# A planned attention and MLP-mixer kernel: first scores of four heads together, pads on VectorE, token mix ahead of the next attention, the last u added by TensorE

## The chip, the cores and the metric

One core of a Trainium2 chip. The metric is the device time of one execution in microseconds (us). A profile shows a span some 2 us shorter than the time of the same execution; both are used below and told apart. For each execution the records give the mean clock that TensorE (PE) was granted, as a share of full speed.

## The reference, cut to what matters

```python
# q, k, v: (8, 8, 576, 64); block-causal mask in blocks of 64 positions
scores = scale * np.matmul(q, k.transpose(0, 1, 3, 2))
scores = np.where(block_i >= block_j, scores, -1e9)
attn = softmax(scores)
x = concat_heads(np.matmul(attn, v))                      # (8, 576, 512)
# mixer
h  = np.maximum(x.transpose(0, 2, 1) @ w_tok1, 0) @ w_tok2     # 576 -> 256 -> 576
u  = x + h.transpose(0, 2, 1)
return u + np.maximum(u @ w_ch1, 0) @ w_ch2                    # 512 -> 1536 -> 512
```

Batch by batch: attention gives x, the *token mix* gives u, the *channel mix* gives the output. 576 rows are four and a half tiles of 128, so the half tiles of two batches are joined into "mixed" tiles (`um`, `gm`). The mixed tile of the last two batches is the last work of the kernel.

## The kernel before

Every operation is handed to a planner (`Plan`). It holds a cost model, a priority per operation (lower first) and the pools of PSUM banks, and fixes, when the program is built, the order in which each engine runs its instructions. At run time each engine goes through its list in order. So a changed priority or cost can move instructions that the diff doesn't touch.

PSUM holds two score buffers of two banks each (`sc`), each used by one score pass at a time, and four banks for everything else (`mm`):

```python
    sc = ring(2, [128, 2, 512], FP32, "sc", psum)
    mm = ring(4, [128, 512], FP32, "mm", psum)
    ...
    WARM, KEEP = 16, 110
```

Constant parts of buffers are written once ("pads"). Those of v are on POOL (GpSimd), which also issues many of the loads:

```python
        for i in range(2):
            fill(
                "POOL", ("v", i), 3.0 + i,
                (v1[i][64:128, 4, :, :], 0.0),
                (v1[i][:, 0:4, :, 64:65], 1.0),
                (v1[i][0:64, 4, :, 64:65], 1.0),
            )
            fill("DVE", ("e", i), -1e3, (e_sb[i][:, :, 1536:1600], 0.0))
```

PE multiplies zeros while it has nothing to do: 16 matmuls at the start, then up to 110 *dummy matmuls*, each placed only if the planner finds a free bank of `mm` and an idle PE before 20 us. 13 of them find a place:

```python
        for n in range(KEEP):
            # one 256-column matmul on zeros into a bank of mm
            P.add("PE", 0.11, emit, pads["zeros"], 1e6, take=[(BANK, bank)], give=[bank], at=5.0 + 0.12 * n, until=20.0)
```

The attention of batch 0 handles two heads at a time (j = 0 to 3), each in three score passes:

```python
        for j in range(4):
            ...
            tails = first_tail(hg, heads, ready[hg], prio + 0.05)
            for n, s in enumerate((2, 1, 0)):
                op = score_set(0, parts, heads, ready[hg], prio + 0.1 * n, [note])   # 4 or 8 matmuls, one sc buffer
                ex = exp(dst, width, op, note, prio + 0.1 * n, urgent=2)             # ACT, 1024 wide
                exps.append(ex)
                for c in MASKS[s]:
                    exps.append(mask(e, c, hs, [ex], prio, urgent=1))                # DVE
```

The last block (the mixed tile of the last two batches) runs in two halves of 256 columns. Each has its own bank, an add of u on VectorE (DVE), and two stores of 64 KB:

```python
    def last_down(gt, ut, deps, prio):
        for f in range(2):
            cols = slice(256 * f, 256 * f + 256)
            # 12 matmuls of 256 columns into a bank
            op = P.add("PE", mm_cost(256, NDC), emit, deps + reuse(("o", f)), prio + 0.1 * f, take=[(BANK, bank)])
            # DVE: o_sb[f][:, 0, 0:256] = bank + ut[:, cols]
            op = P.add("DVE", dve_cost(256), emit, [op], prio, give=[bank])
            for kk in range(2):
                # store 64 rows x 256 columns, on SP's queue for kk = 0, on ACT's for kk = 1
```

The softmax here doesn't subtract the row's maximum and nothing guards it: scores larger than these inputs give would overflow.

## Time and profile before

| | before |
|---|---|
| time, median (4 runs of the comparison) | 314.57 us (314.33 to 315.25) |
| span in the profile, granted clock | 312.5 us, 0.996 |
| first score matmul to last exponential of batch 0 | 8.16 to 20.96 us |
| first 8-matmul scores of batch 1 on PE ("front" ends) | 27.77 us |
| from there to the start of PE's last block ("middle") | 276.85 us |
| from there to the end of the span ("tail") | 7.87 us |

The three last rows sum to the span: 27.77 + 276.85 + 7.87 = 312.49. The lines of the profile are shown in the prediction.

### The profile page before, as it was taken

What the parts mean: (1) busy time and instruction counts of PE and PEld (TensorE: products, weight loads), DVE (VectorE), ACT (ScalarE), POOL (GpSimd) and SP (SyncE); (2) the same over time, 40 slices, a digit from 0 to 9 for tenths busy, and PEclk for the clock granted to TensorE, in tenths of its full rate; (3) what the DMA queues carried; (4) which work ended last, traced back from release to release, by engine and by line L of the source; (5) the groups of instructions that cost most, each with busy time, mean ns of one, the idle gap of its engine ahead of it and who ended that gap; (6) DMA issues with size and microseconds to landing.
All of it is one profiled execution on the core that took longest, in us unless ns stands there. A gap on an engine that the chain in (4) does not pass through costs nothing.

```text
span 312.5 us, 7109 instructions
## 1 busy us (share of the span) xinstructions
PE 299.8 (96%) x2979; PEld 155.3 (50%) x3011; DVE 161.1 (52%) x374; ACT 163.3 (52%) x230; POOL 64.5 (21%) x102
## 2 busy tenths in 40 slices
PE   8898999999999999999999999999999999999993
PEld 3474436454555554553553556544444644444642
DVE  6967739798696586597393753434024022011022
ACT  4875872577757756758646867104504503604500
POOL 7966436612601502500400000000000000000000
PEclk9999999999999999999999999999999999999998
DMA  7999999997995998930890003032311313011013
GB/s 237 173 178 207 205 223 185 230 199 121 103 142 92 125 146 126 216 24 15 81 136 35 36 2 67 2 134 52 67 67 68 69 67 101 2 67 67 2 67 102
DMA packets 57023, 33.12 MB, mean 106 GB/s; under 512 B 43872, under 2 KB 47584, under 8 KB 56992
## 3 DMA queue, kind: packets, MB, share of 16 engines
q0 software_dynamic: 36960, 18.52, 45.3%
q1 hardware_dynamic: 19584, 13.44, 16.3%
q10 hardware_dynamic: 448, 0.72, 0.7%
q8 instruction: 23, 0.38, 0.5%
q14 instruction: 8, 0.07, 0.1%
HBM read 35.85 MB, written 9.44 MB: 145 GB/s over the span
## 4 chain that ended last, share of the span: by engine, by line
PE 64%; issue 12%; DVE 6%; DMA 5%; POOL 2%; POOLq 0%; DVEq 0%
PE mm L943 24%; PE mm L842 23%; PE sc L448 5%; PE mm L496 3%; PE mm L750 3%; DMA qraw<-in_q_dram 3%; PE mm L656 3%; PE mm L869 3%; DMA v<-in_v_dram 2%; DVE x_sb L524 1%; DVE kT L348 1%; DVE o_sb L959 1%; DMA out_dram<-o_sb 1%; POOL kraw L326 1%; POOL qraw L326 1%
## 5 line engine op out<-in xcount | busy, mean ns | idle before, releaser
L468 ACT ACTIVATE e_sb<-sc 128x1024 bf16<-128x1024 f32 x96 | 93.3, 1025 | 35.1 <-PE sc L448 33.1
L842 PE MATMUL mm<-uT,wc_sb 128*128 128x512 bf16 x384 | 88.9, 379 | 0.8 <-DVE u_sb L771 0.4
L943 PE MATMUL mm<-wc_sb,gT 128*128 128x512 bf16 x366 | 85.7, 379 | 1.8 <-issue 0.6
L642 ACT ACTIVATE gT<-mm 128x512 bf16<-128x512 f32 x76 | 45.4, 597 | 70.9 <-PE mm L842 70.7
L959 DVE TENSOR_TENSOR o_sb<-mm,u_sb 128x512 f32<-128x512 f32 x32 | 22.1, 690 | 83.5 <-PE mm L943 83.4
L842 PEld LDWEIGHTS <-wc_sb 128*128 128x128 bf16 x384 | 36.4, 98 | 46.3 <-issue 4.9
L943 PEld LDWEIGHTS <-gT 128*128 128x128 bf16 x384 | 36.0, 98 | 43.7 <-issue 4.1
L448 PE MATMUL sc<-qT,kT 32*128 32x64 bf16 (+4 forms) x752 | 36.3, 281 | 2.1 <-DVE qT L348 1.1
L496 PEld LDWEIGHTS <-e_sb 128*128 128x128 bf16 x896 | 31.1, 97 | 9.3 <-issue 4.8
L496 PE MATMUL mm<-v,e_sb 128*128 128x65 bf16 x896 | 33.4, 193 | 0.2
L377 POOL DMA_DIRECT2D v<-in_v_dram x30 | 25.3, 862 | 33.1 <-PE mm L496 30.9
L524 DVE TENSOR_TENSOR x_sb<-mm,rinv 128x320 bf16<-128x320 f32 x64 | 30.5, 488 | 1.4
L771 DVE TENSOR_TENSOR u_sb<-mm,x_sb 128x512 bf16<-128x512 f32 x32 | 20.6, 684 | 7.5 <-PE mm L750 3.7
L448 PEld LDWEIGHTS <-kT 32*128 32x128 bf16 x752 | 12.9, 93 | 20.3 <-issue 17.0
L348 DVE STREAM_TRANSPOSE kT<-kraw 128x576 int32<-128x576 int32 (+1 forms) x20 | 20.1, 1026 | 4.6 <-PE sc L448 3.0
L348 DVE STREAM_TRANSPOSE qT<-qraw 128x576 int32<-128x576 int32 (+1 forms) x20 | 20.1, 1025 | 0.5 <-DMA qraw<-in_q_dram 0.3
L644 DVE TENSOR_SCALAR gT<-mm 128x512 bf16<-128x512 f32 x20 | 13.7, 687 | 12.6 <-PE mm L842 12.4
L750 PE MATMUL mm<-aT,w_sb 128*128 128x512 bf16 x72 | 19.2, 380 | 0.3 <-DVE e_sb L474 0.2
L656 PE MATMUL mm<-x_sb,w_sb 128*128 128x512 bf16 (+1 forms) x99 | 17.9, 314 | 0.5 <-DVE x_sb L524 0.2
L326 POOL DMA_DIRECT2D kraw<-in_k_dram x15 | 8.4, 559 | 38.0 <-DVE kT L348 21.8
L474 DVE MEMSET e_sb<- 64x128 uint32 (+1 forms) x72 | 10.6, 153 | 9.7 <-ACT e_sb L468 6.1
L642 ACT ACTIVATE aT<-mm 128x512 bf16<-128x512 f32 (+1 forms) x15 | 8.1, 540 | 13.9 <-PE mm L656 13.9
(66 smaller groups left out, 182.1 us busy)
## 6 DMA issues: line engine op xcount, KB each, us to landing
out_dram<-o_sb SPq DMA_DIRECT2D x16, 512.0 KB, 2.8
kraw<-in_k_dram POOLq DMA_DIRECT2D x15, 288.0 KB, 6.3
qraw<-in_q_dram POOLq DMA_DIRECT2D x15, 288.0 KB, 6.6
v<-in_v_dram POOLq DMA_DIRECT2D x24, 128.0 KB, 5.5
wc_sb<-in_moe_w_ch_dram POOLq DMA_DIRECT2D x8, 192.0 KB, 7.8
wc_sb<-in_moe_w_ch_dram POOLq DMA_DIRECT2D x3, 512.0 KB, 11.2
gT<-in_v_dram POOLq DMA_DIRECT2D x9, 128.0 KB, 6.0
gT<-in_v_dram POOLq DMA_DIRECT2D x4, 256.0 KB, 13.3
```

Source lines behind the costliest of these rows:

```text
L348: nc.vector.transpose(dst[:, 0:S, :] .rearrange("p s e -> p (s e)") .bitcast(I32) .rearrange("p (a k) -> p k a", k=NB)[:, k0:k1], raw2.bit ...
L377: nc.gpsimd.dma_start(out=dst, in_=src)
L448: nc.tensor.matmul(out=sc[SC.index(notes[n // 2]["pool"])][:, n % 2, c0 : c0 + w], lhsT=kT[i][r, j0 : j0 + 128, par], rhs=qT[i][r, i0 : i0 ...
L468: nc.scalar.activation(dst, sc[SC.index(note["pool"])][:, :, 0:n], EXP, scale=scale)
L496: nc.tensor.matmul(out=u[:, I, 0:65], lhsT=w, rhs=vt[:, J, head, 0:65], start=(J == 0), stop=(J == I),)
L524: nc.vector.tensor_tensor(out=xt[:, :, 64 * head : 64 * head + 64], in0=u[:, :, 0:64], in1=ri.to_broadcast([128, 5, 64]), op=MULT,)
L642: nc.scalar.activation(dst, src, RELU)
L656: nc.tensor.matmul(out=bank_of(bank)[:, w * n : w * n + w], lhsT=wt[:, 128 * tt : 128 * (tt + 1)], rhs=xt[:, c, cols], start=(c == 0), sto ...
L750: nc.tensor.matmul(out=bank_of(bank), lhsT=w2_sb[:, t, c0 : c0 + 128], rhs=at[:, t, :], start=(t == 0), stop=(t == NDT - 1),)
L842: nc.tensor.matmul(out=bank_of(bank), lhsT=wc1_sb[:, m, 128 * cc : 128 * (cc + 1)], rhs=uT[b % 2][:, :, m, :], start=(m == 0), stop=(m == ...
L943: nc.tensor.matmul(out=bank_of(bank), lhsT=gt[:, cc, c0 : c0 + 128], rhs=wc2_sb[:, cc, :], start=(cc == 0), stop=(cc == NDC - 1),)
L959: nc.vector.tensor_tensor(out=o_sb[oi][:, n % 2, :], in0=bank_of(bank), in1=ut if mixed else ut[:, si, :], op=ADD,)
```

## The change

Its intent: batch 0's attention, where ACT is the engine that sets the pace, should start with more scores ready; POOL should issue loads instead of writing constants; the token mix of a batch should come before the next batch's attention in PE's order; and the end should not wait for an output buffer.

```diff
@@ init_tiles @@
             fill(
-                "POOL", ("v", i), 3.0 + i,
+                "DVE", ("v", i), -60 + 20 * i,
...
-            fill("DVE", ("e", i), -1e3, (e_sb[i][:, :, 1536:1600], 0.0))
+            fill("DVE", ("e", i), -70, (e_sb[i][:, :, 1536:1600], 0.0))
... (the other pads on DVE likewise: -1e3 becomes -70)
@@ Plan: a bank can be given back without the planner's usual lag; the dummies do @@
-                    heapq.heappush(gives, (o.end + lag, note["pool"], note["slot"]))
+                    heapq.heappush(gives, (o.end + lag * (not o.quick), note["pool"], note["slot"]))
...
             P.add(
                 "PE", 0.11, emit, pads["zeros"], 1e6, take=[(BANK, bank)], give=[bank], at=5.0 + 0.12 * n, until=20.0,
+                quick=True,
             )
@@ first_attention: first pass for four heads, heads 2 and 3 into banks of mm @@
-            tails = first_tail(hg, heads, ready[hg], prio + 0.05)
...
+                if j == 0 and n == 0:
+                    note = {}
+                    early = [{}, {}]
+                    op = score_set(
+                        0, parts, range(4), ready[hg], prio - 0.05, [(SC, note)] + [(BANK, x) for x in early]
+                    )
+                if j == 1 and n == 0:
+                    these = []
+                    for h, x in zip(heads, early):
+                        # ACT: one exponential of 512 from bank x
+                        these.append(P.add("ACT", act_cost(512), emit, [op0], prio, give=[x], urgent=2))
...
+                if n == (1 if j else 2):
+                    tails = first_tail(hg, heads, [op] + ready[hg], prio + 0.1 * n + 0.05)
... (one cast of the first k moves to the engine that the planner picks; load costs restated;
     the exponentials of the tails get the priority -3001)
@@ token_mix @@
-        prio = -500 + 10 * b
+        prio = -990.5 + 10 * b
...
-            prio = 1
+            prio = 0.5
@@ last_down: one bank of 512 columns, u added by TensorE @@
+            nc.tensor.matmul(out=bank_of(bank), lhsT=ident, rhs=ut, start=True, stop=False)
+            for cc in range(NDC):
+                nc.tensor.matmul(out=bank_of(bank), lhsT=gt[:, cc, :], rhs=wc2_sb[:, cc, :],
+                                 start=False, stop=(cc == NDC - 1))
...
+        oi = out_n[0] % 3                       # the third output buffer, free long before
+        for f, engine in enumerate(EVAC):       # two copies of 256 columns, DVE and ACT
+            cast(o, o_sb[oi][:, 0, cols], bank_of(bank)[:, cols])
+        for kk in range(2):                     # two stores of 128 KB instead of four of 64 KB
+            queue.dma_start(out=out[B - 2 + kk, 512:576, :], in_=o_sb[oi][64 * kk : 64 * kk + 64, 0, :])
```

## The prediction

> **What bounds the kernel now.** I read four views in this order: the busy shares on the profile page, the busy time of the engines in three stretches, the order of instructions in time at both ends, and the list of what TensorE (PE) waited for.
>
> The page's first part, then the stretches (columns: stretch in us, its length, busy us of PE, PEld, DVE, ACT and POOL, granted clock, DMA share, GB/s):
>
> ```profile
> PE 299.8 (96%) x2979; PEld 155.3 (50%) x3011; DVE 161.1 (52%) x374; ACT 163.3 (52%) x230; POOL 64.5 (21%) x102
> ...
> 20.00:28.00 8.00, 6.83 (x128) 5.63 (x128) 5.76 (x16) 4.22 (x9) 3.80 (x8) 1.00 1.13 205
> 28.00:305.00 277.00, 272.90 (x2651) 139.09 (x2675) 138.58 (x304) 144.46 (x198) 43.65 (x61) 1.00 0.60 97
> 305.00:313.00 8.00, 2.40 (x23) 1.91 (x20) 1.42 (x3) 0.00 (x0) 0.00 (x0) 0.82 0.31 99
> ```
>
> From 28 to 305 us PE is busy 272.9 of 277 us at full clock; no other engine is above 53% there. So the time is three pieces: a front of 28 us until PE is full, a middle that is PE's own stream plus 4.1 us of gaps, and a tail of 8 us. Busy PE in the first 20 us is no proof of useful work (dummy matmuls on zeros are counted), so I looked at the front in order of time (start, length, engine, line, what, idle time before it and its releaser):
>
> ```profile
> 10.74 1.80 POOL L250 MEMSET v<- 64x528 bf16 x6
> 12.52 2.02 POOL L396 DMA_DIRECT2D w_sb<-in_moe_w_tok_dram  x3
> ...
> 17.05 3.91 ACT L468 ACTIVATE e_sb<-sc 128x1024 bf16<-128x1024 f32 x4
> 17.74 0.59 POOL L326 DMA_DIRECT2D qraw<-in_q_dram  x1
> ...
> 24.93 1.26 DVE L348 STREAM_TRANSPOSE kT<-kraw 128x288 int32<-128x288 int32 x2 [0.88 <-DMA kraw<-in_k_dram]
> 26.45 1.26 DVE L348 STREAM_TRANSPOSE qT<-qraw 128x288 int32<-128x288 int32 x2 [0.27 <-DMA qraw<-in_q_dram]
> 27.56 0.68 DVE L717 CAST uT<-mm 128x512 bf16<-128x512 f32 x1
> 27.77 0.63 PE L448 MATMUL sc<-qT,kT 32*128 32x512 bf16 x8 [1.12 <-DVE qT L348]
> ```
>
> The reader is to see two chains. ACT runs exponentials without a gap from 8.83 to 20.96 us; what follows (values, token mix of batch 0) ends on PE at 26.65. Then PE stands 1.12 us because the next scores, which come first in its fixed order, need the q of batch 1. That load was issued at 17.74 and is in only at about 26.4. Behind q's transposes on DVE the last uT copy starts at 27.56 too. The loads are late because POOL, which issues them, spent 10.74 to 12.54 on six memsets, and the DMA engines ran dry behind it:
>
> ```profile
> 12.00:13.00 1.00, 0.97 (x16) 0.49 (x16) 0.90 (x3) 1.00 (x4) 0.94 (x4) 1.00 0.58 115
> 13.00:14.00 1.00, 0.67 (x11) 0.23 (x11) 0.90 (x6) 1.00 (x3) 1.00 (x3) 1.00 0.05 10
> 14.00:15.00 1.00, 0.88 (x20) 0.61 (x20) 0.90 (x4) 1.00 (x3) 0.93 (x3) 1.00 1.01 129
> ```
>
> Before and after this hole the DMA share is 1.0 or more, so the hole, (1-0.58)+(1-0.05) = 1.4 us, is pushed onto every later load. The tail:
>
> ```profile
> 304.62 2.78 PE L899 MATMUL mm<-wc_sb,gmT 128*128 128x256 bf16 x24
> 306.13 0.42 DVE L910 TENSOR_TENSOR o_sb<-mm,um_sb 128x256 f32<-128x256 f32 x1 [0.56 <-PE mm L899]
> 306.59 2.94 ACTq L918 DMA_DIRECT2D out_dram<-o_sb  x2
> 308.57 0.42 DVE L910 TENSOR_TENSOR o_sb<-mm,um_sb 128x256 f32<-128x256 f32 x1 [2.02 <-DMA out_dram<-o_sb]
> ```
>
> PE has finished at 307.40, yet the last add starts at 308.57: its output buffer is still being written out by the store before. That wait is 1.1 us.
>
> **What the Trainium skill says.** "TensorE: Matmul & The Clock Gate", Back-to-back issue gap, gives N/2.4 ns plus 2.5 ns for a warm matmul, 216 ns for 512 columns. The trace agrees: four of these take 0.86 us in the chain of work. Its section Part 3 says matmuls start and end in program order, and that four 32-row tiles run together; the trace has eight 512-column score matmuls of four heads in 0.63 us against 0.62 for four matmuls of two heads. "ScalarE: Activation LUTs", What ACT_TABLE_LOAD costs, has a fixed part and 0.833 ns an element, and about 93 ns of overlap back to back; here 1025 ns for 1024 elements, with starts about 0.92 apart. "PSUM — Partial Sum Buffer", PSUM bank collisions raise a hardware error, says two engines may not touch one bank and partition quadrant at once, two readers included. No trace here shows that, but the built program's waits do: the new tail's VectorE half waits for the ScalarE half.
>
> **The change part by part.**
>
> 1. *Pads on VectorE.* POOL loses 1.80 us of memsets, so the weight loads and k and q of batch 1 are issued up to 1.8 us earlier. The DMA can use at most the 1.4 us hole. q then lands near 25.0. DVE gets six memsets: two of 264 words (0.27 each, as a 256-word memset took) and four small ones (about 0.1), 0.95 us, from 3.40 to 4.35. DVE's next task begins at 5.47 (in the new order the k transpose), so this costs nothing. New DVE order at 24 us: the last normalisation ends at 24.05, k transposes to 25.4, q transposes to 26.65, just when PE ends the token mix. Scores start at about 26.75 instead of 27.77: **-1.0 us**, bounded below by DVE and not by the load.
>
> 2. *First scores for four heads, two in pool banks.* It removes one score pass of two heads (0.6 us) from PE, where PE waits anyway. ACT is what this stage runs on, and one exponential of 1024 becomes two of 512: 2 x (0.597-0.10) = 1.0 against 0.92, **+0.08 us**. The first one waits for 16 matmuls instead of 8, but four row groups run together: +0.02. The moved k cast (now ScalarE) ends near 6.05, when the other half's transpose ends at 6.10, and q arrives at 6.11: zero. In the new order every score pass has its bank a full exponential before ACT needs it, so no gap on ACT. Stage: **+0.1 us**.
>
> 3. *Token mix ahead of the next attention.* It moves work on PE and adds none. By the built order the score groups from the second batch on number 49 in both kernels. Each costs about 0.25 us above its arithmetic (a pass of 8 is 0.57 in the chain against 0.43, and the block after it starts 0.11 late), so equal counts mean equal cost. All that can move are the waits in the middle. Those over 0.15 us sum to 2.3 us, eleven of 0.16 to 0.40, mostly on x_sb or u_sb of DVE. Ten second-layer token matmuls now mostly run in one piece; an earlier token mix gives uT more time, but blocks of four banks now fill faster. I choose **-0.3 us**, give or take 0.8.
>
> 4. *Last u on TensorE.* PE's last block: 24 x 0.109 + 0.163 = 2.78 becomes 13 x 0.2157 + 0.163 = 2.97, +0.19; it ends at 307.59 on the old clock. Then ScalarE copies 256 columns (0.384 as for aT of that size), a hand-over of 0.07, VectorE copies 256 (about 0.42): with 0.06 to start, 308.52 against 308.99 before. The output buffer is now the third one, free long ago. -0.47. Each store carries 128 KB instead of 64; the page's stores of 128 KB land in 2.4 us, those of 64 KB in 2.0 and 2.3: +0.2. **-0.3 us**.
>
> Sum: -1.0 + 0.1 - 0.3 - 0.3 = -1.5 us. In the timed runs 314.5 - 1.5 = **313.0 us**, 0.5% less.
>
> **Rivals.** (a) *The wait for q turns into another one.* New q loads share queues with the channel weights and v. If the DMA takes the hole's gain away, q still lands at 26.4 and nothing is won: about 314.0. For it: share above 1.0 from 15 us on, all of it a backlog. Against it: a backlog without the hole is simply earlier. (b) *The ACT chain stretches.* If one of the new bank hand-overs comes late, or the ten extra dummy matmuls (23 instead of 13, 0.11 us each, in PE's order ahead of scores) delay a score pass, ACT stands and everything behind it with it: +0.5 to +1, 313.5 to 314. Against it: six or seven dummies are 0.75 us, and the passes behind them wait for an exponential that takes longer. (c) *The reordered middle is the main effect.* If most of the 4.1 us of gaps goes, 310.5 to 311; if the new fixed order makes PE wait for DVE, which has more to do just after a token mix, 314 to 315. Against both: no wait in the old middle exceeds 0.4 us, so there is little to win, and the same planner made both orders. (d) *The tail gains its whole 1.1 us*, if the two half copies overlapped: 0.4 less. The waits of the built program speak against it.
>
> **Range and chances.** The front is worth 0 to -1.4, the tail 0 to -0.9, the middle -1.5 to +1. Together 311.4 to 314.5 should hold it 8 times in 10. Over 2% faster would need 308.2 or less: front, tail and every gap of the middle at once, 2%. Over 2% slower would need 6 us of new waits on PE: 1%. Within 2%: 97%.
>
> **What would show it.** Right, if: POOL's token-weight loads start near 10.7; the DMA share has no hole at 12 to 14 us; the first eight-matmul scores start near 26.8 with under 0.3 us idle before them; ACT is gapless to about 21.1; PE is busy all but 3 to 4.5 us in the 277 us that follow; the last copy ends 0.9 us after PE, and no store is waited for before it. Wrong, if scores of batch 1 still wait for q, if ACT has gaps before 21 us, or if any wait of PE in the middle exceeds 0.5 us.

## The result, and the profile after

The changed kernel took 313.40 us (median of 4 runs, 313.15 to 313.82) against 314.57 us (4 runs, 314.33 to 315.25). The ratio is 0.9961, with a 95% interval of 0.9942 to 0.998. A ratio is the mean time of one kernel's fast runs over that of the other's of the same rounds, so not quite the ratio of the medians; the record calls the two the same within 2%. The four runs of the changed kernel were at a granted clock of 0.996 or more. For the four of the kernel before no clock is on record, but their times are those of its full-clock runs elsewhere (314.49 to 315.37), and its profiled run was at 0.996. The prediction was 313.0 us in a range of 311.4 to 314.5: right in size and direction. Its steps fared less well, and that the sum fits is in part luck: the middle gave 0.37 us more than predicted, the tail 0.73 and the front 0.28 less.

The page's first line and the three stretches, after (columns as in the prediction: stretch, length, busy us of PE, PEld, DVE, ACT and POOL, granted clock, DMA share, GB/s):

```profile
PE 302.3 (97%) x3010; PEld 154.7 (50%) x3010; DVE 159.4 (51%) x377; ACT 164.8 (53%) x234; POOL 63.1 (20%) x96
...
20.00:28.00 8.00, 7.63 (x135) 5.94 (x135) 5.82 (x15) 4.99 (x12) 4.17 (x7) 1.00 1.15 208
28.00:305.00 277.00, 275.51 (x2678) 139.19 (x2677) 138.03 (x302) 144.78 (x199) 43.31 (x60) 1.00 0.60 96
305.00:313.00 8.00, 1.30 (x7) 0.39 (x4) 0.42 (x1) 0.37 (x1) 0.00 (x0) 0.81 0.30 99
```

PE now stands 1.5 us in the middle stretch. The page before showed 4.1 us, but 2.6 us of that were never there. In the record before, the loads of weights and the matmuls differ in number (3011 against 2979), so 32 matmuls are missing: 20 of the 420 of the channel mix's second layer, 8 of 80 of the token mix's, and four more. In the record after, none is missing. The experiment p1_pads below runs the matmuls of the kernel before in the same order (but for two dummies), with a complete record: in this stretch its PE is busy 275.50 us. So PE stood 1.5 us before as well. A share of PE read from a page is a lower bound.

The cut into three pieces says where the time went:

| us | before | after | difference | predicted |
|---|---|---|---|---|
| front: to the first 8-matmul scores of batch 1 | 27.77 | 27.15 | -0.62 | -0.9 (pads -1.0, scores +0.1) |
| middle: to the start of PE's last block | 276.85 | 276.18 | -0.67 | -0.3 |
| tail: to the end of the span | 7.87 | 8.30 | +0.43 | -0.3 |
| sum | 312.49 | 311.63 | -0.86 | -1.5 |

The profiles show 0.86 of the 1.17 us between the medians: the profiled run of the kernel before took 314.27 us, less than each of its four timed ones. In a second profile of the changed kernel (a_again below) the middle and the tail are the same, but the front is 27.59 us, only 0.18 us shorter than before.

**The hole in the DMA** is gone. The same two stretches as in the prediction, after:

```profile
12.00:13.00 1.00, 1.00 (x12) 0.61 (x10) 1.00 (x2) 1.00 (x4) 1.00 (x3) 1.00 0.97 128
13.00:14.00 1.00, 1.00 (x27) 0.69 (x24) 0.83 (x6) 1.00 (x2) 0.93 (x3) 1.00 1.37 192
```

The shares were 0.58 and 0.05; they are 0.97 and 1.37.

**The front in order of time**, after (start, length, engine, line, what, idle time before it and its releaser):

```profile
10.92 2.04 POOL L397 DMA_DIRECT2D w_sb<-in_moe_w_tok_dram  x3
...
16.29 0.58 POOL L329 DMA_DIRECT2D qraw<-in_q_dram  x1
...
17.40 3.05 ACT L479 ACTIVATE e_sb<-sc 128x1024 bf16<-128x1024 f32 x3
...
20.55 1.05 ACT L479 ACTIVATE e_sb<-sc 128x1024 bf16<-128x1024 f32 x1
...
24.43 1.26 DVE L349 STREAM_TRANSPOSE kT<-kraw 128x288 int32<-128x288 int32 x2 [0.23 <-DMA kraw<-in_k_dram]
25.84 1.26 DVE L349 STREAM_TRANSPOSE qT<-qraw 128x288 int32<-128x288 int32 x2 [0.15 <-DMA qraw<-in_q_dram]
26.93 0.68 DVE L749 CAST uT<-mm 128x512 bf16<-128x512 f32 x1
27.15 0.64 PE L460 MATMUL sc<-qT,kT 32*128 32x512 bf16 x8 [0.36 <-DVE qT L349]
```

The token weights are issued 1.60 us earlier (12.52 to 10.92) and q 1.45 us earlier (17.74 to 16.29). But q's transposes start only 0.61 us earlier (26.45 to 25.84), because DVE still waits for the loads: 0.23 us for that of k, then 0.15 us for that of q. The predicted start of the scores was 26.75 us; they start at 27.15, still 0.36 us behind q. ACT ends its last exponential at 21.60 instead of 20.96.

**The tail**, after:

```profile
303.33 0.38 PE L929 MATMUL mm<-um_sb,ident 128*128 128x512 bf16 x1
303.55 2.75 PE L931 MATMUL mm<-wc_sb,gmT 128*128 128x512 bf16 x12
306.33 0.37 ACT L309 COPY o_sb<-mm 128x256 f32<-128x256 f32 x1 [12.57 <-PE mm L931]
306.74 0.42 DVE L311 COPY o_sb<-mm 128x256 f32<-128x256 f32 x1 [2.46 <-ACT o_sb L309]
307.19 0.47 SPq L954 DMA_DIRECT2D out_dram<-o_sb  x1
307.20 0.55 ACTq L954 DMA_DIRECT2D out_dram<-o_sb  x1
```

No store is waited for any more, and the last copy ends 0.87 us after PE, as predicted. What follows the copy is longer than before. The pieces of the tail, in us:

| | PE's last block | to the last copy's end | to the last byte landed | to the end of the span | sum |
|---|---|---|---|---|---|
| before | 2.78 | 1.59 | 2.28 | 1.22 | 7.87 |
| after | 2.97 | 0.87 | 2.66 | 1.81 | 8.30 |

**Waits of PE**, after (line waited for; us in total, times, longest):

```profile
PE sc L460 <- DVE qT L349: 0.8, 2, 0.4
PE mm L507 <- DVE uT L852: 0.7, 1, 0.7
...
PE mm L688 <- DVE x_sb L535: 0.3, 2, 0.2
```

In the middle there is one wait above 0.5 us, which the prediction had named as a sign of being wrong: values of a later batch stand 0.7 us for a bank that DVE copies uT from. All that PE stands in the middle is still no more than before (step 3 below).

### The profile page after: what moved, and what is told of

It is laid out like the page before. It is cut to its first block, busy times and chain, and to the rows that moved or that the text cites. A ratio compares the mean times of both kernels' runs of the same rounds, so it can differ in the third digit from the quotient of the medians.

```text
span 311.6 us, 7140 instructions
## 1 busy us (share of the span) xinstructions
PE 302.3 (97%) x3010; PEld 154.7 (50%) x3010; DVE 159.4 (51%) x377; ACT 164.8 (53%) x234; POOL 63.1 (20%) x96
## 4 chain that ended last, share of the span: by engine, by line
PE 83%; DMA 5%; DVE 5%; POOL 3%; issue 2%; ACT 0%; POOLq 0%
PE mm L979 29%; PE mm L874 27%; PE sc L460 7%; PE mm L507 7%; PE mm L688 5%; PE mm L782 4%; PE mm L901 4%; DMA qraw<-in_q_dram 3%; DMA kraw<-in_k_dram 2%; DVE x_sb L535 1%; DVE u_sb L803 1%; POOL gT L378 1%; PE mm L931 1%; POOL wc_sb L416 1%; POOL w_sb L397 1%
## 5 line engine op out<-in xcount | busy, mean ns | idle before, releaser
L979 PE MATMUL mm<-wc_sb,gT 128*128 128x512 bf16 x384 | 89.1, 379 | 0.0
L674 ACT ACTIVATE gT<-mm 128x512 bf16<-128x512 f32 x74 | 44.2, 597 | 60.4 <-PE mm L874 60.3
L979 PEld LDWEIGHTS <-gT 128*128 128x128 bf16 x384 | 35.3, 98 | 42.5 <-issue 4.3
L460 PE MATMUL sc<-qT,kT 32*128 32x320 bf16 (+4 forms) x744 | 35.9, 281 | 0.9 <-DVE qT L349 0.8
L676 DVE TENSOR_SCALAR gT<-mm 128x512 bf16<-128x512 f32 x22 | 15.1, 688 | 15.3 <-PE mm L874 15.3
L674 ACT ACTIVATE aT<-mm 128x512 bf16<-128x512 f32 (+1 forms) x17 | 9.3, 547 | 16.7 <-PE mm L688 16.5
```

Source lines behind the costliest of these rows:

```text
L460: nc.tensor.matmul(out=home(n)[:, c0 : c0 + w], lhsT=kT[i][r, j0 : j0 + 128, par], rhs=qT[i][r, i0 : i0 + w, par], start=(par == 0), stop= ...
L674: nc.scalar.activation(dst, src, RELU)
L979: nc.tensor.matmul(out=bank_of(bank), lhsT=gt[:, cc, c0 : c0 + 128], rhs=wc2_sb[:, cc, :], start=(cc == 0), stop=(cc == NDC - 1),)
```

## The experiments

Ten kernels ran, all with correct results. The chips of these runs put most executions of the kernel before into a low-clock state that the first comparison had not shown, so three comparisons stand beside each other: the reported ratio (which mixes clocks), the mean of the full-clock runs, and the pieces of the profile. Where a profile fell into the low-clock state, only its front was slow: in the four such profiles the full clock is back at 26.3 to 30.4 us, before batch 1's scores. So middles and tails may be compared across all runs. Kernel before in the same sessions: first session full-clock mean 314.65 us (4 of 11 runs), second 315.09 (1 of 11), third 314.97 (5 of 11).

The theory, as the prediction has it: four parts, each worth its own amount, which add up. The rival: the planner's whole order decides, so a part alone is worth something else than in company. The first four runs apply one part each to the kernel before.

### p1_pads: pads alone

```diff
-                "POOL", ("v", i), 3.0 + i,
+                "DVE", ("v", i), -60 + 20 * i,
... (other pads: -1e3 becomes -70, cost 0.2 becomes 0.17)
```

> The kernel before with only the pads moved to VectorE; PE's order is unchanged. Theory (the hole in the loads is filled, but the last of the 16 DMA engines keeps part of the gain): token-weight loads start near 10.9 us, no hole in the DMA share at 12 to 14 us, first eight-matmul scores of batch 1 near 27.1 instead of 27.77, and 0.4 to 0.7 us off the time. Rival (the loads are a backlog anyway and the hole is made up): scores stay within 0.15 us of 27.77 and the time within 0.15 us of the kernel before.

Measured: median 314.11 us, ratio 0.9943 (0.9876 to 1.0009); full-clock runs 313.80 (4 of 6) against 314.65, so -0.85 us. The front, from its profile in order of time:

```profile
25.07 1.23 DVE L348 STREAM_TRANSPOSE qT<-qraw 128x288 int32<-128x288 int32 x2
...
26.58 0.63 PE L448 MATMUL sc<-qT,kT 32*128 32x512 bf16 x8
```

No wait is left in either line: q is in before DVE wants it, the scores start at 26.58, 1.19 us earlier than before. The middle is that of before (276.83), the tail 8.22. So the mechanism of step 1 (POOL's memsets, the hole, q, the scores) holds, and it is worth slightly more than predicted when it stands alone, and more than was expected of this run.

### p2_mix: token mix ahead, alone

```diff
-        prio = -500 + 10 * b
+        prio = -990.5 + 10 * b
...
-            prio = 1
+            prio = 0.5
```

> The kernel before with only the two priorities of the token mix changed. Theory (the middle's gain of 0.67 us, start of batch 1's scores to start of PE's last block, comes from the order): this stretch shrinks from 276.85 to 276.0 to 276.5 us and the time by 0.3 to 0.8. Rival (the gain comes from loads and scores that are earlier, or is noise): within 0.15 us of 276.85.

Measured: median 318.64 us, ratio 1.0072 (1.0006 to 1.0139), but five of its six runs were at low clock. The one at full clock took 315.89 us, +1.2. The middle of its profile (a low-clock one, at full clock again from 26.3 us on) is 277.49 us: 0.64 us *longer* than before. The priority alone does not shorten the middle; neither the theory nor the rival of this run had foreseen that it lengthens it.

### p3_tail: the new last block alone

```diff
-        for f in range(2):
-            ... 12 matmuls of 256 columns, add on DVE, two stores of 64 KB
+        ... ident x ut, 12 matmuls of 512 columns, two copies, two stores of 128 KB, third output buffer
```

> The kernel before with only the tail changed. Theory (what the wait for the output buffer gives, the 128 KB stores and what follows their landing take back): last copy ends 0.5 us earlier after the start of PE's last block than in the kernel before, but the stores land about 0.4 us later after it and the closing takes 0.2 to 0.6 longer; the time is 0.0 to 0.5 us up. Rival (the prediction): 0.3 us down.

Measured: median 318.31 us, ratio 1.0082 (1.0025 to 1.0139); all six runs at low clock. Four of them at 0.979 to 0.984 average 318.2 us, where the kernel before has 317.4 at the same clocks (5 runs of that session): +0.8. Its tail is 2.97 + 0.87 + 2.64 + 1.80 = 8.28 us, the pieces of after to 0.02 us. So the new tail is not shorter than that of before: 0.4 us longer than in the profile before, and as long as the mean of the four profiles with the old tail (8.33, see step 4 below). What the +0.8 us consist of is open.

This kernel differs from the one before only in its last 8 us, and its middle is that of before (276.88 us). Its profile therefore shows what a low-clock run of that front looks like. The clock row of the two pages (forty slices of the span, tenths of full speed), first after, then this kernel:

```profile
PEclk9999999999999999999999999999999999999998
```

```profile
PEclk9756999999999999999999999999999999999999
```

and two stretches of the front of this kernel (columns as above):

```profile
8.00:12.00 4.00, 1.91 (x30) 1.01 (x30) 3.59 (x8) 2.53 (x6) 2.96 (x5) 1.00 0.97 209
12.00:20.00 8.00, 8.00 (x81) 3.73 (x81) 4.71 (x20) 6.60 (x11) 7.76 (x18) 0.50 0.78 120
```

From 8 to 12 us PE worked 1.91 of 4 us; from 12.0 us on it runs at half clock for 17.1 us by the clock record of the trace. Its scores of batch 1 start at 34.03 us instead of 27.77.

### p4_scores: four heads first, alone (with the quick dummies)

```diff
+                if j == 0 and n == 0:
+                    op = score_set(0, parts, range(4), ready[hg], prio - 0.05, [(SC, note)] + [(BANK, x) for x in early])
... (tails after the passes, casts, load costs and quick=True as in the change)
```

> The changed kernel with pads, token mix priority and tail as before, so only the first scores of four heads, the cast assignment and the extra dummies. Theory (ScalarE's chain is longer by one fixed part and the start is a little later): last exponential of batch 0 ends 0.1 to 0.4 us later than 20.96, scores of batch 1 still wait for q near 27.7, time within 0.4 us of the kernel before either way (the middle's order differs too). Rival (four heads at once shorten the stage): last exponential ends before 20.8.

Measured: median 316.36 us, ratio 1.0008 (0.9955 to 1.0062); full-clock runs 316.08 (4 of 6) against 314.65, so +1.4 us. From its profile in order of time:

```profile
17.70 3.05 ACT L479 ACTIVATE e_sb<-sc 128x1024 bf16<-128x1024 f32 x3 [0.47 <-PE sc L460]
...
28.68 0.64 PE L460 MATMUL sc<-qT,kT 32*128 32x512 bf16 x8 [1.59 <-DVE qT L349]
```

ACT stands 0.47 us for a score pass, and its exponentials end at 21.90 instead of 20.96. With the memsets still on POOL, q was last to land at 27.34 and PE stands 1.59 us for it. The middle is 277.25 (+0.40), and its tail is the longest of all, 8.95 us, although it is built like the one before: the stores took 2.95 us to land and the closing 1.63. This profile was of a run at 316.65 us, the slowest at full clock. The chain of exponentials and the time both missed what was expected (0.1 to 0.4 us later; within 0.4 us).

The four single parts at the best comparison each allows: -0.85, +1.2, +0.8 and +1.4. They sum to +2.6 us, and all together measured -1.2. Three of the four are weak: the +1.2 rests on one run at full clock, the +0.8 on runs at low clock, and up to 1.1 us of the +1.4 can be a tail that this part did not change. But the pieces that are free of this do not add up either: the middles alone differ by -0.02, +0.64, +0.03 and +0.40, and by -0.67 together. The theory that the parts add up has fallen; the rival stands.

### a_again: the changed kernel once more

> The changed kernel itself, word for word, on the same chip as the next ones. Theory (the ten extra dummy matmuls keep TensorE's clock up through the front): all or nearly all of its runs at a granted clock of 0.99 or more, near 313.4 us, while a part of the runs of the kernel before fall to 0.97 to 0.985 and 317 to 319 us. Rival (the half clock strikes either kernel alike): as many low runs as the kernel before.

No edit. Measured on another chip: median 313.09 us, six of six runs at full clock; ratio 0.9852 (0.9813 to 0.9891), because the kernel before had ten of its eleven runs below 0.995 there (median 317.50). Pieces: front 27.59, middle 276.16, tail 8.29. The middle and the tail repeat to 0.02 us. The front does not: PE stood 0.7 us for q this time (0.36 in the first profile).

### a_noquick: changed kernel, dummies give their bank back with the usual lag

```diff
-                quick=True,
+                quick=False,
```

> The changed kernel with the banks of the dummy matmuls given back as late as before, so 16 dummies instead of 23; nothing else in any engine's order moves. Theory (dummies hold the clock): some runs at 0.97 to 0.985 and 317 us or more, as the kernel before; the others within 0.3 us of the changed kernel. Rival (dummies only delay PE): no low runs, and up to 0.3 us faster than the changed kernel.

Fewer dummies find a place (16 instead of 23). Measured: median 313.85 us, ratio 0.9891 (0.9838 to 0.9944); five of six runs at full clock, mean 313.73 against 313.17 for the changed kernel in the same session (0.3 had been expected at most), and one run at 317.72 (0.974); one low run in six against none in six decides nothing. Pieces 27.23, 276.17, 8.30: the same plan in all that matters. The seven extra dummies cost nothing that shows; rival (b) of the prediction, that they delay the score passes, is refuted in the direction that it named.

### t1_halves: changed kernel, two halves for the last block again, but in the free buffer

```diff
+        oi = out_n[0] % 3
+        o_war = reuse(("o", oi))
         for f in range(2):
             ... 12 matmuls of 256 columns
-                    out=o_sb[f][:, 0, 0:256], in0=bank_of(bank)[:, 0:256], in1=ut[:, cols], op=ADD
+                    out=o_sb[oi][:, f, 0:256], in0=bank_of(bank)[:, 0:256], in1=ut[:, cols], op=ADD
             ... two stores of 64 KB
```

(shown against the last block of the kernel before; the rest is the changed kernel)

> The changed kernel with the tail of the kernel before (two half blocks of 256 columns, u added by VectorE, 64 KB stores) but in the free output buffer. Theory (the wait for the buffer was all that was to be won; the 128 KB stores and the two copies in a row cost it again): PE's last block 2.78 us, last add 0.5 us after it, stores 2.3, so the span ends 0.7 to 1.3 us earlier than the changed kernel's after the start of the last block, 0.6 to 1.3 us faster in runs of like clock. Rival (u on TensorE is the gain): slower than the changed kernel or the same within 0.2 us.

Measured: median 311.52 us (311.26 to 311.76), six of six at full clock; 1.65 us under the changed kernel of the same session by the means. Its tail in order of time:

```profile
303.24 2.78 PE L933 MATMUL mm<-wc_sb,gmT 128*128 128x256 bf16 x24
...
304.75 0.42 DVE L944 TENSOR_TENSOR o_sb<-mm,um_sb 128x256 f32<-128x256 f32 x1 [0.56 <-PE mm L933]
305.21 1.78 SPq L952 DMA_DIRECT2D out_dram<-o_sb  x2
305.21 1.81 ACTq L952 DMA_DIRECT2D out_dram<-o_sb  x2
306.06 0.42 DVE L944 TENSOR_TENSOR o_sb<-mm,um_sb 128x256 f32<-128x256 f32 x1 [0.89 <-PE mm L933]
```

In the session's comparison with the kernel before the ratio is 0.98 (0.9762 to 0.9839), which the record calls unclear, since the interval reaches to either side of 2%. The second add now follows PE at once (0.89 us idle, ended by PE, where the profile before had 2.02 ended by a store). Pieces 2.78 + 0.46 + 2.27 + 1.20 = 6.72 against 8.29: -1.57 of the 1.65 measured, where 0.6 to 1.3 had been expected. The wait for the buffer is what the old tail lost. Adding u on TensorE took that wait away by the way and gave back what it won: in two halves the first add and its stores run while PE works on the second half, in one block of 512 columns all copies and stores come behind PE.

### best: the kernel before with pads, quick dummies and these halves

```diff
 kernel before
+ pads as in p1_pads, quick=True for the dummies, last block as in t1_halves
```

> The kernel before with three things: pads on VectorE, the tail in two halves in the free output buffer, and dummy banks given back at once (15 dummies). No four-head scores, no token mix moved. Theory (pads and the buffer are the whole of the gain): batch 1's scores start near 26.6, tail 6.6 to 7.2 us, 1.5 to 2.2 us off the kernel before and 0.3 to 1.0 us under the changed kernel in runs of like clock. Rival (four-head scores and the moved token mix carry the gain): slower than the changed kernel.

Measured: median 312.81 us, ratio 0.9881 (0.9818 to 0.9944); full-clock runs 312.46 (4 of 6), two runs near 316.4. Pieces 26.64, 276.88, 6.87. Its front is 0.44 us better than that of t1_halves, its middle 0.71 worse. So the new order on PE (token mix and four heads) is worth having once the pads are moved, and this shorter edit is not the best version. Against the changed kernel it is 0.7 us faster, as expected; that pads and buffer are the whole of the gain is refuted by t1_halves, which is faster still by 0.94 us.

### t2_nokeep: changed kernel without any dummies

```diff
-    WARM, KEEP = 16, 110
+    WARM, KEEP = 16, 0
```

> The changed kernel without any of the 23 dummy matmuls between the first scores (the 16 at the very start stay); no other order moves but two DVE entries. Theory (the dummies hold TensorE's clock): most of its runs at a granted clock under 0.99 and at 316 us or more. Rival (what keeps the clock is the four-head order, not the dummies): all runs at 0.99 or more, within 0.3 us of 313.1.

Measured: median 317.49 us; eight of eight runs at low clock (0.964 to 0.975), where the changed kernel had ten of ten at 0.996 or more. The clock row of its page, and stretches of its front:

```profile
PEclk9655999999999999999999999999999999999998
```

```profile
8.00:9.00 1.00, 0.00 (x0) 0.00 (x0) 0.00 (x0) 0.08 (x1) 0.00 (x0) 1.00 1.03 216
10.00:11.00 1.00, 0.03 (x4) 0.03 (x7) 1.00 (x3) 0.17 (x1) 1.00 (x2) 0.50 0.58 141
11.00:12.00 1.00, 1.00 (x22) 0.83 (x23) 1.00 (x3) 0.00 (x0) 1.00 (x3) 0.50 0.73 197
```

Nothing runs on PE from 8 to 9 us, and by 10 us it is granted half its clock, just as its work begins. The middle (276.16) and the tail (8.30) are those of the changed kernel; all of the loss is in the front, whose scores of batch 1 start at 34.88 us. In this profile and in that of p3_tail the first score was late as well (10.97 and 9.50 us, against 8.0 to 8.4 in the full-clock profiles), because the first q came late; in the low-clock profiles of p2_mix and c1_twohead it was not (8.20 and 8.22). A late load is therefore not needed for the clock to fall, but it leaves PE idle in the same way as missing dummies do.

### c1_twohead: t1_halves with the first attention of the kernel before

```diff
 t1_halves
- four heads in the first pass, tails late
+ two heads in the first pass, tails first (kernel before)
```

> The changed kernel with the tail in two halves in the free buffer (as in the experiment before) and with the first attention of the kernel before: scores two heads at a time, tails first; it has 15 dummies. Theory (four heads at once lengthen ScalarE's chain and give nothing): last exponential ends near 21.0 instead of 21.7, first scores of batch 1 near 26.6 to 26.8; but some runs fall to a low clock, as with every kernel of 13 to 16 dummies. At like clock within 0.4 us of the two-halves kernel's 311.5. Rival (four heads at once carry the front): batch 1's scores later than 27.1 and over 0.4 us slower at like clock.

Measured: median 313.71 us, ratio 0.9884 (0.9811 to 0.9956). Three of six runs at full clock, mean 311.65 us, against 311.52 for t1_halves in another session; the other three between 315.56 and 317.81. The middle is 276.39. Its profile fell into the low clock, so what was expected of its front could not be read. At the same clock the four-head pass is thus worth about nothing; what came with it, banks free for 23 dummies instead of 15, is the subject of the next table.

### All runs by their dummies

| dummies placed | kernels | runs at low clock (below 0.99) |
|---|---|---|
| 0 | t2_nokeep | 8 of 8 |
| 13 | before (first comparison, judged by the times; the three sessions of the experiments) | 0 of 4; 22 of 33 |
| 13 | p1_pads, p2_mix, p3_tail | 13 of 18 |
| 15 or 16 | best, c1_twohead, a_noquick | 6 of 18 |
| 23 | after and a_again, t1_halves | 0 of 16 |
| 23 | p4_scores | 1 of 6, at 0.989 |

Where PE stands still in the front differs as well. From the traces, each gap of PE over 0.5 us between its first matmul and 18 us (start and length, us), with the clock of that profile:

```
before       9.31 0.59                full
p1_pads      9.47 0.60                full
best         7.52 0.86, 9.53 0.59     full
p2_mix       9.35 0.59                half from 16.0
c1_twohead   7.12 1.10, 9.37 0.59     half from 11.2
p3_tail      7.54 1.96, 10.65 0.59    half from 12.0
t2_nokeep    7.42 3.55                half from 9.9
after        none                     full
a_again      7.14 1.03, 15.95 0.60    full
t1_halves    7.64 0.59, 15.95 0.56    full
a_noquick    7.51 0.55, 15.86 0.58    full
p4_scores    16.12 0.59               full
```

With four heads first and dummies, the wait near 9.4 us is filled (the last five rows), though most of these profiles have one near 16 us instead. The gaps alone don't tell kept from lost: with one of 0.59 us the clock was kept in one profile (before) and lost in another (p2_mix), and a_again kept it with one of 1.03 us.

The last dummy in PE's order ran at 11.7 us in the kernel before and at 15.0 us in the changed one. The split by dummies is between kernels that differ in other things too, except for t2_nokeep and a_noquick, which change nothing else but the place of two or three entries of other engines; and the first comparison, with the kernel before at full clock four times out of four, shows that the chip or the moment has a say.

## Why the prediction was right or wrong, point by point

**What bounds the kernel: right.** Front, middle and tail were the right pieces, and no engine but PE bounds the middle. The size of the gaps was not: PE stood 1.5 us in the middle and not 4.1; the rest were matmul records missing from the trace. They spoil the list of waits too: the 2.3 us in eleven waits over 0.15 us are 1.04 us in four by the complete record of p1_pads.

**Step 1, pads on VectorE: the mechanism right, "bounded below by DVE and not by the load" wrong in the changed kernel.** The issues came earlier by 1.4 to 1.6 us and the hole vanished, as the step says; alone (p1_pads) the scores started 1.19 us earlier. In the changed kernel the whole front gained 0.62 us (0.18 in a_again, 0.69 in t1_halves), because loads came late: that of k at 24.40, for which DVE stood 0.23 us, and that of q at 25.81 instead of near 25.0. In a_again k was in time and q cost all of it (DVE stood 0.79 us for it). The completions of the load of q, which come from 16 DMA engines one by one, show how (us at which the 14th, 15th and 16th came in, from the traces):

```
             14th    15th    16th
before       25.92   26.28   26.43
p1_pads      24.20   24.23   24.94
after        24.60   25.80   25.81
a_again      24.48   24.59   26.26
t1_halves    24.74   25.17   25.75
a_noquick    24.48   24.77   25.89
```

In the changed kernel 14 of 16 parts were there by 24.60; the load is late by its last one or two parts. Before batch 1's scores each trace has two packets of 16 KB in the queue that carries instructions, in the changed kernel's first profile at 16.40 (1.33 us long) and 23.74 (0.94 us). In this profile, from the first of them on, the last part of every load is 1.1 to 1.8 us behind the one before it, and behind the second packet a second part is late. In a_again no part is late behind the first packet (16.13), only behind the second. The Trainium skill, "Runtime: NRT & Kernel Launch", section Instruction fetch mechanics, says that an engine's instructions are refilled in blocks of 16 KiB by DMA, the cost "mostly hidden"; the size agrees with the packets here. That such a fetch holds up the part of the load that shares its DMA engine fits in size and mostly in time (in a_again the second fetch began at 24.21 and the last part came at 26.26), but no run moved a fetch, so it is argued and not shown.

**Step 2, four heads: "no gap on ACT" wrong, its sum about right.** ACT stood for a score pass (0.13 to 0.47 us at a time in the full-clock profiles with this pass), and its chain ended 0.64 to 0.77 us later in the changed kernel where +0.1 had been predicted (after and a_again). The token mix on PE, which had slack behind that chain, ended only 0.13 to 0.27 us later (26.78 and 26.92 against 26.65). By c1_twohead, four heads or two make no difference of time at full clock that shows between two sessions.

**Step 3, the token mix: the sum within its margin, the mechanism wrong.** Predicted -0.3 give or take 0.8, out of the waits, since the step "moves work on PE and adds none". The middle lost 0.67 us, and did so to 0.02 us in five profiles with this plan. But it did not come out of the waits. Where the record of matmuls is complete, PE stands 1.50 to 1.54 us in the middle of the old order (p1_pads, p3_tail, best) and 1.49 to 1.50 us in that of the new one. What fell is its busy time in the middle, from 275.33 to 275.36 us before to 274.66 to 274.69 us. So the same matmuls took 0.65 us less in the new order; "equal counts mean equal cost" is the premise that failed. The sign of being wrong, a wait over 0.5 us, came true (0.7), and many short gaps went. The priority, the named cause, made the middle 0.64 us longer alone, by more standing (2.25 us). With pads and quick dummies beside it (c1_twohead against best, which also differ in the cast of the first k and in the planner's costs of loads) it took off 0.49, and the four heads another 0.2. So the gain belongs to the plan and not to one line. Which matmuls got shorter, and by which of the planner's choices, stays open.

**Step 4, the last block: this step failed.** -0.3 was predicted, the profiles say +0.43. PE's +0.19 and the 0.87 us to the last copy's end (0.93 predicted) were right. Two terms behind the copy were not. The stores of 128 KB landed in 2.66 instead of 2.28 us, +0.38 where +0.2 had been taken; and from the last byte landed to the end of the span it took 1.81 instead of 1.22, +0.59 where nothing had been taken. The second term came out as 1.80 or 1.81 in all five profiles with this tail. The traces show what it consists of: SP works off a list of waits for semaphores, most of them long reached, at some 0.07 us each. With the new tail two more of them lie behind the last landing, and one step takes 0.49 us in all five profiles; why that one does is open (p2_mix and p4_scores, with the old tail, have such a step too). Part of the shortfall is the reference: the 7.87 us of the kernel before are the shortest of four profiles with its tail (7.87, 8.22, 8.29, 8.95; mean 8.33). Against that mean the new tail is worth nothing either way. t1_halves shows what the step overlooked: the same buffer with two halves ends 1.57 us earlier.

**The rivals.** (a), the wait for q stays, came half true. (b), ACT's chain stretches and the ten extra dummies delay PE: the chain stretched, the dummies delayed nothing. What (b) missed is what the dummies are for. (c), the middle as the main effect, is near: it was the larger of the two gains, by 0.05 us in the first profile and by 0.51 in a_again; but it did not come out of the gaps, as (c) has it. (d) fell.

**What was not foreseen at all: the clock.** The prediction took the clock of the one profile as given. In the sessions of the experiments the kernel before lost it in 22 of 33 runs, and the changed kernel in none of ten. A low-clock run of the kernel before costs 2.5 to 6 us (317.1 to 320.8 against 314.7 to 315.1). In the session in which it was at full clock only once in eleven runs, the change was worth 1.5% (ratio 0.9852) instead of 0.4%. The Trainium skill, "TensorE: Matmul & The Clock Gate", section What's actually happening, says that the array's default state is half clock, that activity lifts it, and that this is judged in windows of about 3.4 us. The traces agree: the stretches shown have 1.00 or 0.50, and by the clock records the half clock lasted 10.24 us in p2_mix, 17.07 in p3_tail and c1_twohead and 20.48 in t2_nokeep, which is 3, 5 and 6 times 3.41 us. The first rise to full clock comes 4.3 to 6.9 us after the start, so the windows lie differently over the same instructions in each execution. That this makes the loss a matter of chance is argued and not tested. The page's later section HAM oscillation gives idle gaps over 3.4 us as what brings the half clock back; here gaps of 0.6 to 2 us went with it in three profiles of four. In the last 3.41 us before the fall PE was busy 76% (p2_mix), 69% (c1_twohead), 56% (p3_tail) and 27% (t2_nokeep); but p4_scores kept the full clock after such a window with 53%, so busy time alone draws no line. How little work in a window is enough to lose the clock was not measured.

**The version that beats both** is t1_halves: 311.52 us, six runs of six at full clock, 1.65 us under the changed kernel (ratio of the means 0.9947), and 2.0% under the kernel before as that ran in the same session (interval 1.6 to 2.4%), most of it by the clock.

**Left open:** what delays the last parts of a load, which matmuls of the middle got shorter and by which choices of the planner, p3_tail's loss at low clock, the long step in the closing, and where the store of p4_scores lost 0.7 us.

## What to carry to other kernels

When a planner fixes the order, test the parts together and in pairs: four parts that measured -0.85, +1.2, +0.8 and +1.4 us alone were worth -1.2 together. A wait for a buffer at the end is cured by another buffer; keep the halves whose copies and stores overlap with the rest of the work. And look at the granted clock of many runs before trusting one: work on zeros that keeps PE busy through the front cost nothing measurable here, and all of it or none (a_again, t2_nokeep) decided between 313 us in every run and 317 us or more in all but two. Count the matmul records of a trace against its loads of weights before reading gaps from it.

## What the Trainium skill lacked or had wrong

- "TensorE: Matmul & The Clock Gate", What's actually happening, puts the penalty of the clock's ramp, that is of the half clock at the start, under 1% of a typical span. That section has no figure for losing the clock again in the front of a kernel: here, in 314 us, that cost 2.5 to 6 us, 0.8 to 1.8%, and varied from run to run of one program: 22 of 33 runs of the kernel before had it, none of ten of the changed one.
- The same page, HAM oscillation, has idle gaps over 3.4 us bring the half clock back. Here the clock was lost with no gap of PE longer than 1.10 us (c1_twohead) and even 0.59 us (p2_mix). The page's section after that one tells of short idle times between groups of matmuls that do it as well, but gives no amount. 0 dummy matmuls gave 8 low-clock runs of 8, 15 or 16 gave 6 of 18, and 23 gave 0 of 16 in the changed kernel and t1_halves.
- "Runtime: NRT & Kernel Launch", Instruction fetch mechanics, has the fetches "mostly hidden". The 16 KB packets in the front here took 0.9 to 1.7 us each, and in the changed kernel's profiles the loads behind one of them had a part of their 16 in up to 1.8 us late; whether the one causes the other was not tested.
- No page that I found gives what a kernel's own end costs. From the last byte landed to the last of the program's instructions it took 1.19 to 1.81 us here, and depended on the last stores: 1.80 or 1.81 in all five profiles with two of 128 KB, 1.19 to 1.65 with four of 64 KB.
- No page that I read warns that records of matmuls are missing in a trace unevenly: 32 of 3011 in one, none in the other, so that PE's busy time in the middle stretch differs by 2.6 us between the two pages, where the middle itself differs by 0.67.
